# Spreading ScalarE's work over a loop, and one low half in four by TensorE and ScalarE in three stages

## The chip, the cores and the metric

The kernel runs on one core of a Trainium2 chip. The metric is the device time of one execution in microseconds (us); before the change the median of three runs is 1210.32 us (1210.09 to 1211.27).

## What is computed

A dynamic convolution over the sequence, followed by a mixture of experts with one expert per token. There are 8 x 3584 = 28672 tokens of 192 features.

```python
w = softmax(weight_gen)                       # per token and head: 7 taps
conv[b, s, h] = sum_k w[b, s, h, k] * x_pad[b, s + k, h]   # 8 heads of 24 features
logits = conv @ w_gate                        # 8 experts
e = argmax(logits);  gate = softmax(logits)[e]
out = gate * (relu(conv @ w1[e]) @ w2[e])     # 192 -> 1024 -> 192
```

## The kernel before

**Two halves of a pipeline.** The tokens are cut into 16 chunks of 14 x 128. A *producer* takes a chunk `c` through the convolution on VectorE: 14 multiplications by a tap's weight (L401) and 12 additions (L406), each over half a chunk. For the chunk before, it scales the result to float16 rows (`tops` L415 on ScalarE makes the high part, `halves` L428 on VectorE subtracts it to get the low part), transposes them on TensorE (`turn`, L442, copied out by ScalarE at L443), multiplies by the gate (`products`, L451) and routes: `route1` finds the expert and the counts, `counts` takes the exponential (L492), `route2` makes the row positions, and GpSimd scatters the rows to a list per expert in DRAM (L505). The softmax of the next chunk's tap weights (`soft_a`, `soft_e`, `soft_b`) and its size (`size_a`, L199) lie in the same loop. `load_chunk` issues the next chunk's loads on SP and copies the six positions that overlap (the halo, L119) on ScalarE.

A *consumer* works through blocks of 256 rows of one expert (stages 0 and 1 also have blocks of 128); stage `s` holds the lists filled from chunk `s`. A block of 256 has four steps. In a step `first` makes 2 x 128 hidden features with ten matmuls (L689 to L693), ScalarE applies relu and rounds to float16, the high half `hh` (L696). The rounding error, the low half `hl`, is made in one of two ways:

```python
if self.via[k]:
    PE.matmul(p1, lhsT=negi, rhs=hh, start=False, stop=True, skip_group_check=True)
    A.activation(out=hl, in_=p1, func=AF.Relu)
else:
    V.scalar_tensor_tensor(out=hl, in0=p1, scalar=0.0, in1=hh, op0=ALU.max, op1=ALU.subtract)
```

The first way takes a subtracting matmul (L703) and ScalarE (L704), the second VectorE (L706). `second` (L723) multiplies both halves by `w2`: eight matmuls for the high half and four for the low half. The low half is used four steps after its `first`. `NZ[s]` says how many of eight positions use VectorE in stage `s`; of the list `via` (L940) a block of 256 uses the first four entries. NZ is 0 for stages 0 to 4, 5 for stage 5 and 8 (VectorE alone) from there; after the producer's end VectorE takes all.

**What sets the order.** Producer and consumer are generators that yield planned times. The loop at L996 to L1002 goes on with the producer as long as its time `tp`, plus 0.65 us for each low half that VectorE was given (`own`), plus 4 us, is not beyond the consumer's time, and with the consumer otherwise. Each engine gets its instructions in the order in which this loop calls them and runs them in that order. Inside the producer, `o` counts from -1 through 13 pairs of the convolution; the tables `ZERO` to `EARLY` say at which `o` each part stands (in `EARLY`, for chunks from 4 on: tops at -1, halves at 1, turn from 2, products at 4, route1 at 6, counts at 8, route2 at 9, soft_a at 7, soft_b at 10).

Three small operations have two versions, chosen by the chunk's number: the softmax sum's epsilon (L378 on VectorE, L380 on ScalarE), the cast of the counts (L482, L484) and the gate's sum (L519, L521 with L522). On ScalarE they stand from chunk 6 on.

Of the kernel before, what the change touches and what calls it, by code (L numbers as in the profile page):

```python
# [12 lines left out]
AF = mybir.ActivationFunctionType  # L13
# [4 lines left out]
B, S, D = 8, 3584, 192  # L18
# [4 lines left out]
HALO = K - 1  # L23
T = 14
WID = [14] * 16
# [17 lines left out]
SECOND = dict(tops=-1, halves=-1, turn=-1, per=6, products=-1, route1=-1, counts=-1, route2=0, soft_a=6, soft_b=10, size=8)  # L43
END = 2.1
HEAD = 4.0
WARM = (6, 8, 18)
LONE = {1: 6, 2: 2}
WB = 4
# [7 lines left out]
HHB, HLB, YB = 6, 6, 20  # L56
AV, TLOAD, SLOW = 4.0, 12.0, 0.5
SKEW = 4.0
NZ = [0] * 5 + [5] * 1 + [8] * 10
DH = 0.65  # L60
ALWAYS = (6, 3)
REST = P
# [20 lines left out]
def conv_moe_kernel(ctx: ExitStack, tc: tile.TileContext, x, wgen, wg_in, w1, w2, out):  # L83
    nc = tc.nc
    V, A, GP, PE, SP = nc.vector, nc.scalar, nc.gpsimd, nc.tensor, nc.sync
# [15 lines left out]
    nchunk = len(WID)  # L101
# [6 lines left out]
    tin = {}  # L108

    def load_chunk(c):  # L110
        t0, w = at[c], WID[c]
        wgt = small.tile([P, T * H, K], F32, name="wgt")[:, 0:w * H, :]
        SP.dma_start(out=wgt, in_=wgen.rearrange("(p t) h k -> p t (h k)", p=P)[:, t0:t0 + w, :])
        xin = big.tile([P, (T + HALO) * D], F32, name="xin")
        z = HALO if c else 0
        for a, b in ((z, w + HALO),) if c else ((0, X0), (X0, w + HALO)):
            SP.dma_start(out=xin[:, a * D:b * D], in_=x[:, (t0 + a) * D:(t0 + b) * D])
        if c:
            A.activation(func=AF.Copy, out=xin[:, 0:HALO * D], in_=tin[c - 1]["xin"][:, WID[c - 1] * D:(WID[c - 1] + HALO) * D])  # L119
        tin[c] = dict(wgt=wgt, xin=xin)  # L120

    load_chunk(0)
    wgf = const.tile([P, 2, E], F32, name="wgf")
# [248 lines left out]
    def soft_b(c):  # L372
        wgt, n = tin[c]["wgt"], WID[c] * H
        sm = small.tile([P, T * H], F32, name="sm")[:, 0:n]
        V.tensor_reduce(out=sm, in_=wgt, axis=AX.X, op=ALU.add)
        yield 1.0
        if c < 6:
            V.tensor_scalar(out=sm, in0=sm, scalar1=1e-9, scalar2=None, op0=ALU.add)  # L378
        else:
            A.activation(out=sm, in_=sm, func=AF.Copy, bias=1e-9)  # L380
            yield None
        V.reciprocal(out=sm, in_=sm)
        yield 0.9
        V.tensor_tensor(out=wgt, in0=wgt, in1=sm.unsqueeze(2).to_broadcast([P, n, K]), op=ALU.mult)
        yield 1.0
# [71 lines left out]
    def route1(s):  # L457
        d = seg[s]
        n = WID[s]
        pl = d["pl"]  # L460
        with tc.high_priority(offset=PRIO2):
            fac = small.tile([P, 1], F32, name="fac")
            A.activation(out=fac, in_=d["sx"][:, 2:3], func=AF.Copy, scale=wi[:, 2 * E:2 * E + 1])
            lg = work.tile([P, T, E], F32, name="lg")[:, 0:n, :]
            V.tensor_reduce(out=lg, in_=pl[:, 0:16 * n].rearrange("p (t z e) -> p t e z", z=2, e=E), axis=AX.X, op=ALU.add)
            lm = small.tile([P, n], F32, name="lm")
            V.tensor_reduce(out=lm, in_=lg, axis=AX.X, op=ALU.max)
            V.tensor_tensor(out=lg, in0=lg, in1=lm.unsqueeze(2).to_broadcast([P, n, E]), op=ALU.subtract)
            vr = work.tile([P, T, E], F32, name="vr")[:, 0:n, :]
            V.scalar_tensor_tensor(out=vr, in0=lg, scalar=0.0, in1=r8.unsqueeze(1).to_broadcast([P, n, E]), op0=ALU.is_equal, op1=ALU.mult)  # L470
        yield 1.5
        with tc.high_priority(offset=PRIO2):
            ve = small.tile([P, n], F32, name="ve")
            V.tensor_reduce(out=ve, in_=vr, axis=AX.X, op=ALU.max)
            oh = work.tile([P, E * T], F32, name="oh")[:, 0:E * n].rearrange("p (e t) -> p e t", e=E)
            V.tensor_tensor(out=oh.rearrange("p e t -> p t e"), in0=vr, in1=ve.unsqueeze(2).to_broadcast([P, n, E]), op=ALU.is_equal)
            inc = work.tile([P, E * T], F32, name="inc")[:, 0:E * n].rearrange("p (e t) -> p e t", e=E)
            V.tensor_tensor_scan(out=inc.rearrange("p e t -> p (e t)"), data0=scm[n].rearrange("p e t -> p (e t)"),
                                 data1=oh.rearrange("p e t -> p (e t)"), initial=0.0, op0=ALU.mult, op1=ALU.add)
            cnt = small.tile([P, E], F16, name="cnt")  # L480
            if s < 6:
                V.tensor_copy(out=cnt, in_=inc[:, :, n - 1])  # L482
            else:
                A.activation(out=cnt, in_=inc[:, :, n - 1], func=AF.Copy)  # L484
        d.update(lg=lg, oh=oh, inc=inc, cnt=cnt, fac=fac)
        yield 1.1
# [24 lines left out]
    def route2(s):  # L511
# [3 lines left out]
        with tc.high_priority(offset=PRIO2):  # L515
            ge = small.tile([P, n], F32, name="ge")
            V.tensor_reduce(out=ge, in_=lg, axis=AX.X, op=ALU.add)
            if s < 6:
                V.tensor_scalar(out=ge, in0=ge, scalar1=1e-9, scalar2=d["sx"][:, 1:2], op0=ALU.add, op1=ALU.mult)  # L519
            else:  # L520
                A.activation(out=ge, in_=ge, func=AF.Copy, bias=1e-9)  # L521
                A.activation(out=ge, in_=ge, func=AF.Copy, scale=d["sx"][:, 1:2])  # L522
# [258 lines left out]
    def produce():  # L781

        t, ta = 10.0, 0.0
# [21 lines left out]
        for e in range(WB):  # L805
            prep_load(e)
        load_chunk(1)
        SP.dma_start(out=scri[TRASH:TRASH + 256, :].rearrange("(p j) c -> p j c", j=2), in_=zrow.bitcast(I32))
        for _ in soft_b(0):
            pass  # L810
        t += 8
        for c in range(nchunk + 1):
            dt = DT * (WID[c] if c < nchunk else T) / T
            at_o = {0: ZERO, 1: FIRST, 2: SECOND, 3: THIRD}.get(c, EARLY)
            it = conv(c) if c < nchunk else None
            tops_, turn_, products_, size_, soft_ = None, None, None, None, None
            for o in range(-1, OPS + 1 + LONE.get(c, 0) // 2):
# [7 lines left out]
                    yield t  # L825
                if o == (3 if c == 2 else 0) and c and c < nchunk - 1:
                    load_chunk(c + 1)
                if o == at_o["tops"] and c:
                    tops_ = tops(c - 1)
                for _ in range(1 if at_o in (EARLY, THIRD) else 2):  # L830
# [21 lines left out]
                for _ in range(at_o["per"]):  # L852
                    if turn_ and next(turn_, 0):
                        state["pe"] += 0.9
                        ta += 1.1
                if o == at_o["products"] and c:
                    products_ = products(c - 1)
                for _ in range(1 if at_o in (EARLY, THIRD) else 2):
# [18 lines left out]
                if c + 1 < nchunk and c != 1:  # L877
                    if o == at_o["soft_a"]:
                        ta += 1
                        for d in soft_a(c + 1):  # L880
                            t += d
                            yield t
                    if o == at_o["soft_a"] + (0 if c == 0 else 1):
                        soft_e(c + 1)
                    if o == at_o["soft_b"] and c:
                        soft_ = soft_b(c + 1)
                    while soft_ and (d := next(soft_, None)) is not None:
                        t += d
                        yield t
# [3 lines left out]
                if o == at_o["route1"] and c:  # L893
                    for d in route1(c - 1):
                        t += d
                        yield t
                if o == at_o["counts"] and c:
                    counts(c - 1)
                if o == at_o["route2"] and c == 1:
# [129 lines left out]
```

## Time and profile before

| | |
|---|---|
| median of the runs | 1210.32 us |
| profiled execution | 1210.91 us, span 1209.2 us |
| TensorE matmuls, busy | 1128.4 us (93%) |
| VectorE, busy | 1049.2 us (87%) |
| ScalarE, busy | 694.9 us (57%) |
| GpSimd, busy | 759.6 us (63%) |
| low halves by VectorE (L706) | 322, by ScalarE (L704) 134 |

Busy time is a share of the whole span, and the stages differ: the head (to about 130 us) splits the weights, in the stretch to about 480 us low halves are made by TensorE and ScalarE, then to about 1000 us by VectorE beside the convolution, and after it TensorE works on what is left of the blocks. A line number names the instruction's place in the kernel. A wait names the instruction that came last before the waiting one could begin.

### The profile page before, as it was taken

Reading aid. Unit: us, or ns where it says so; the run is one execution under the profiler, and the core shown is the slowest. Engines: PE = TensorE matmul, PEld = TensorE weight load, DVE = VectorE, ACT = ScalarE, POOL = GpSimd, SP = SyncE. Lnnn points to the kernel's source line nnn. Section 1 sums busy time; section 2 is a strip of 40 time slices with the busy share of each in tenths; the row PEclk is TensorE's granted clock in tenths of the full one; section 3 lists DMA queues with packets and bytes.
Section 4 is the critical chain, followed back from the end, with each engine's and each line's share of the span. In section 5 each row is a group of like instructions: output and inputs, shape, how many; then the busy total and the mean of one; then the engine's idle time right before and its main releaser. Section 6 shows DMA issues by size and latency. Waiting matters only on the chain.

```text
span 1209.2 us, 31966 instructions
## 1 busy us (share of the span) xinstructions
PE 1128.4 (93%) x12159; PEld 1014.2 (84%) x12159; DVE 1049.2 (87%) x1416; ACT 694.9 (57%) x1382; POOL 759.6 (63%) x587
## 2 busy tenths in 40 slices
PE   4778888999999999999999999999999999999997
PEld 3343877888878888999989999999999999999997
DVE  7999999999999999999999999999999995533332
ACT  3887657767676776755646464564646446333342
POOL 1434573847686878788838888785867875621222
PEclk9899899999999999999999999999999999999999
DMA  9987999998998999999999999999999899999994
GB/s 300 312 265 244 299 327 299 281 309 271 258 278 223 294 232 275 269 277 281 317 242 316 255 288 281 268 322 253 309 271 263 246 269 252 295 311 254 260 240 157
DMA packets 214064, 331.43 MB, mean 274 GB/s; under 512 B 138382, under 2 KB 157951, under 8 KB 211856
## 3 DMA queue, kind: packets, MB, share of 16 engines
q1 hardware_dynamic: 190752, 282.31, 84.5%
q0 software_dynamic: 21696, 44.99, 12.9%
q10 hardware_dynamic: 1456, 2.03, 0.6%
q8 instruction: 97, 1.59, 0.6%
q14 instruction: 63, 0.52, 0.2%
HBM read 246.39 MB, written 60.83 MB: 254 GB/s over the span
## 4 chain that ended last, share of the span: by engine, by line
DVE 63%; PE 23%; DMA 5%; issue 4%; ACT 3%; POOL 1%; SPq 1%; ACTq 0%; DVEq 0%; POOLq 0%
DVE acc L406 19%; DVE tmp L401 19%; PE po L723 10%; DVE hl L706 8%; DVE acc L401 3%; DVE rows L428 3%; PE p L689 2%; PE p L693 2%; PE p L692 2%; PE p L690 2%; PE p L691 2%; PE p L282 2%; DMA out_dram<-y,mt 1%; POOL out_dram L732 1%; ACT xt L443 1%
## 5 line engine op out<-in xcount | busy, mean ns | idle before, releaser
L732 POOL DMA_INDIRECT out_dram<-y,mt x228 | 318.2, 1396 | 231.1 <-ACT y L731 167.4
L505 POOL DMA_INDIRECT scr<-rows,pos x224 | 345.8, 1544 | 149.2 <-issue 57.6
L696 ACT ACTIVATE hh<-p 128x512 f16<-128x512 f32 x456 | 271.6, 598 | 259.5 <-PE p L693 252.7
L723 PE MATMUL po<-wb,hh 128*128 128x192 f16 x3648 | 359.2, 246 | 1.6 <-ACT hh L696 1.6
L706 DVE SCALAR_TENSOR_TENSOR hl<-p,hh 128x512 f16<-128x512 f32 x322 | 215.2, 678 | 116.0 <-ACT hh L696 115.7
L723 PEld LDWEIGHTS <-hh 128*128 128x128 f16 x3648 | 307.9, 98 | 4.6 <-ACT hh L696 2.2
L401 DVE TENSOR_TENSOR tmp<-xin,wgt 128x1344 f32<-128x1344 f32 x192 | 292.5, 1547 | 1.2
L406 DVE TENSOR_TENSOR acc<-acc,tmp 128x1344 f32<-128x1344 f32 x192 | 292.3, 1546 | 0.4
L689 PE MATMUL p<-xb,wa 128*128 128x256 f16 (+1 forms) x960 | 256.8, 267 | 4.8 <-DMA xb<-scr 3.9
L693 PE MATMUL p<-xb,wa 128*128 128x256 f16 (+1 forms) x960 | 256.9, 268 | 0.0
L692 PE MATMUL p<-xb,wa 128*128 128x256 f16 (+1 forms) x960 | 256.9, 268 | 0.0
L691 PE MATMUL p<-xb,wa 128*128 128x256 f16 (+1 forms) x960 | 256.8, 268 | 0.0
L690 PE MATMUL p<-xb,wa 128*128 128x256 f16 (+1 forms) x960 | 256.8, 268 | 0.0
L723 PE MATMUL po<-wb,hl 128*128 128x192 f16 x1824 | 225.5, 246 | 22.9 <-ACT hl L704 17.9
L723 PEld LDWEIGHTS <-hl 128*128 128x128 f16 x1824 | 160.0, 98 | 36.5 <-ACT hl L704 22.5
L690 PEld LDWEIGHTS <-wa 128*128 128x128 f16 x960 | 94.0, 98 | 18.9 <-issue 1.4
L704 ACT ACTIVATE hl<-p 128x512 f16<-128x512 f32 x134 | 80.9, 604 | 44.4 <-PE p L703 43.7
L689 PEld LDWEIGHTS <-wa 128*128 128x128 f16 x960 | 94.1, 98 | 10.1 <-DMA wa<-wsa 2.7
L693 PEld LDWEIGHTS <-wa 128*128 128x128 f16 x960 | 94.1, 98 | 9.8
L692 PEld LDWEIGHTS <-wa 128*128 128x128 f16 x960 | 94.1, 98 | 9.9
L691 PEld LDWEIGHTS <-wa 128*128 128x128 f16 x960 | 94.0, 98 | 9.8
L443 ACT ACTIVATE xt<-p 128x1024 f16<-128x1024 f16 x96 | 82.3, 926 | 18.7 <-PE p L442 18.6
(147 smaller groups left out, 1087.8 us busy)
## 6 DMA issues: line engine op xcount, KB each, us to landing
wb<-wsb SPq DMA_DIRECT2D x120, 768.5 KB
wa<-wsa SPq DMA_DIRECT2D x120, 768.0 KB
xin<-in_x_dram SPq DMA_DIRECT2D x15, 1344.0 KB
wa<-wsa SPq DMA_DIRECT2D x120, 128.0 KB
wgt<-in_weight_gen_dram SPq DMA_DIRECT2D x16, 392.0 KB
wa<-in_moe_w_dram SPq DMA_DIRECT2D x8, 768.0 KB
wa<-in_moe_w_dram SPq DMA_DIRECT2D x8, 512.0 KB
wsa<-wt SPq DMA_DIRECT2D x15, 256.0 KB
```

The source lines that it names most:

```text
L401: V.tensor_tensor(out=t[:, a:b, :].rearrange("p t (h g) -> p (t h) g", g=G), in0=xv, in1=wv, op=ALU.mult)
L406: V.tensor_tensor(out=acc[:, a:b, :], in0=acc[:, a:b, :], in1=t[:, a:b, :], op=ALU.add)
L505: i = raw(GP.indirect_dma_start(scri, bass.IndirectOffsetOnAxis(ap=pos[:, t:t + 1], axis=0), rows_t[s % 3].bitcast(I32)[:, t, 0:RW // 2], ...
L689: PE.matmul(o, lhsT=wt[:, F + fs:F + fs + P], rhs=xv[:, 0, :], start=i == 0, stop=False)
L690: PE.matmul(o, lhsT=wt[:, F + fs:F + fs + P], rhs=xv[:, 1, :], start=False, stop=False)
L691: PE.matmul(o, lhsT=wt[:, 3 * F + fs:3 * F + fs + P], rhs=xv[:, 0, :], start=False, stop=False)
L692: PE.matmul(o, lhsT=wt[:, 2 * F + fs:2 * F + fs + P], rhs=xv[:, 2, :], start=False, stop=False)
L693: PE.matmul(o, lhsT=wt[:, fs:fs + P], rhs=xv[:, 2, :], start=False, stop=i == self.each - 1)
L696: self.relu = raw(A.activation(out=hh, in_=p1, func=AF.Relu, scale=1.0 - 2.0 ** -11 if self.via[k] else 1.0))
L706: V.scalar_tensor_tensor(out=hl, in0=p1, scalar=0.0, in1=hh, op0=ALU.max, op1=ALU.subtract)
L723: PE.matmul(o, lhsT=h[:, js], rhs=w2, start=(f == 0 and j % 2 == 0 and not part and w == 0), stop=part == 1 and f == NF - 1 and (j % 2 == ...
L732: i = raw(GP.indirect_dma_start(out, bass.IndirectOffsetOnAxis(ap=self.mt[:, j, 1:2], axis=0), y, None, bounds_check=N - 1, oob_is_err=False))
```

## The change

The halo copy leaves `load_chunk` for a function of its own, called at `o` = 8. Before the tops, after each part of the turn and before the counts, from chunk 3 on, the producer yields a time 1.2 us later than its own, so that consumer steps may come first in the order. The exponential of the tap weights goes one place later from chunk 4 on. The three small operations stay on VectorE through chunk 7. In stages 11 to 13, `NZ` is 7 instead of 8: the first of a block's four low halves goes by L703 and L704.

```diff
@@ -43,6 +43,8 @@
 SECOND = dict(tops=-1, halves=-1, turn=-1, per=6, products=-1, route1=-1, counts=-1, route2=0, soft_a=6, soft_b=10, size=8)
 END = 2.1
 HEAD = 4.0
+HALO_AT = 8
+MORE = 1.2
 WARM = (6, 8, 18)
 LONE = {1: 6, 2: 2}
 WB = 4
@@ -56,7 +58,7 @@
 HHB, HLB, YB = 6, 6, 20
 AV, TLOAD, SLOW = 4.0, 12.0, 0.5
 SKEW = 4.0
-NZ = [0] * 5 + [5] * 1 + [8] * 10
+NZ = [0] * 5 + [5] * 1 + [8] * 5 + [7] * 3 + [8] * 2
 DH = 0.65
 ALWAYS = (6, 3)
 REST = P
@@ -115,9 +117,10 @@
         z = HALO if c else 0
         for a, b in ((z, w + HALO),) if c else ((0, X0), (X0, w + HALO)):
             SP.dma_start(out=xin[:, a * D:b * D], in_=x[:, (t0 + a) * D:(t0 + b) * D])
-        if c:
-            A.activation(func=AF.Copy, out=xin[:, 0:HALO * D], in_=tin[c - 1]["xin"][:, WID[c - 1] * D:(WID[c - 1] + HALO) * D])
         tin[c] = dict(wgt=wgt, xin=xin)
+
+    def load_halo(c):
+        A.activation(func=AF.Copy, out=tin[c]["xin"][:, 0:HALO * D], in_=tin[c - 1]["xin"][:, WID[c - 1] * D:(WID[c - 1] + HALO) * D])
 
     load_chunk(0)
     wgf = const.tile([P, 2, E], F32, name="wgf")
@@ -374,7 +377,7 @@
         sm = small.tile([P, T * H], F32, name="sm")[:, 0:n]
         V.tensor_reduce(out=sm, in_=wgt, axis=AX.X, op=ALU.add)
         yield 1.0
-        if c < 6:
+        if c < 8:
             V.tensor_scalar(out=sm, in0=sm, scalar1=1e-9, scalar2=None, op0=ALU.add)
         else:
             A.activation(out=sm, in_=sm, func=AF.Copy, bias=1e-9)
@@ -478,7 +481,7 @@
             V.tensor_tensor_scan(out=inc.rearrange("p e t -> p (e t)"), data0=scm[n].rearrange("p e t -> p (e t)"),
                                  data1=oh.rearrange("p e t -> p (e t)"), initial=0.0, op0=ALU.mult, op1=ALU.add)
             cnt = small.tile([P, E], F16, name="cnt")
-            if s < 6:
+            if s < 8:
                 V.tensor_copy(out=cnt, in_=inc[:, :, n - 1])
             else:
                 A.activation(out=cnt, in_=inc[:, :, n - 1], func=AF.Copy)
@@ -515,7 +518,7 @@
         with tc.high_priority(offset=PRIO2):
             ge = small.tile([P, n], F32, name="ge")
             V.tensor_reduce(out=ge, in_=lg, axis=AX.X, op=ALU.add)
-            if s < 6:
+            if s < 8:
                 V.tensor_scalar(out=ge, in0=ge, scalar1=1e-9, scalar2=d["sx"][:, 1:2], op0=ALU.add, op1=ALU.mult)
             else:
                 A.activation(out=ge, in_=ge, func=AF.Copy, bias=1e-9)
@@ -805,6 +808,7 @@
         for e in range(WB):
             prep_load(e)
         load_chunk(1)
+        load_halo(1)
         SP.dma_start(out=scri[TRASH:TRASH + 256, :].rearrange("(p j) c -> p j c", j=2), in_=zrow.bitcast(I32))
         for _ in soft_b(0):
             pass
@@ -825,6 +829,10 @@
                     yield t
                 if o == (3 if c == 2 else 0) and c and c < nchunk - 1:
                     load_chunk(c + 1)
+                if o == HALO_AT and c and c < nchunk - 1:
+                    load_halo(c + 1)
+                if o == at_o["tops"] and c > 2:
+                    yield t + MORE
                 if o == at_o["tops"] and c:
                     tops_ = tops(c - 1)
                 for _ in range(1 if at_o in (EARLY, THIRD) else 2):
@@ -853,6 +861,8 @@
                     if turn_ and next(turn_, 0):
                         state["pe"] += 0.9
                         ta += 1.1
+                        if c > 2:
+                            yield t + 1.2
                 if o == at_o["products"] and c:
                     products_ = products(c - 1)
                 for _ in range(1 if at_o in (EARLY, THIRD) else 2):
@@ -880,7 +890,7 @@
                         for d in soft_a(c + 1):
                             t += d
                             yield t
-                    if o == at_o["soft_a"] + (0 if c == 0 else 1):
+                    if o == at_o["soft_a"] + (0 if c == 0 else 1 if c < 4 else 2):
                         soft_e(c + 1)
                     if o == at_o["soft_b"] and c:
                         soft_ = soft_b(c + 1)
@@ -894,6 +904,8 @@
                     for d in route1(c - 1):
                         t += d
                         yield t
+                if o == at_o["counts"] and c > 2:
+                    yield t + MORE
                 if o == at_o["counts"] and c:
                     counts(c - 1)
                 if o == at_o["route2"] and c == 1:
```

The instruction orders show what moves. Line numbers of the changed kernel are 3 higher behind its new function. The first place is ScalarE at the tops (`rows`) of one of the steady chunks, at the end of its convolution. Before:

```order
L366 ACTIVATE sx<-ll 128x1
L415 ACTIVATE rows_1248<-acc,sx 128x14x128
L696 ACTIVATE hh<-p_12603 128x512
L119 ACTIVATE xin<-xin 128x1152
L415 ACTIVATE rows_1248<-acc,sx 128x14x64
L696 ACTIVATE hh<-p_12637 128x512
L681 ACTIVATE g_12656<-mt,wb_1250 128x2
```

and now:

```order
L369 ACTIVATE sx<-ll 128x1
L699 ACTIVATE hh<-p_12597 128x512
L418 ACTIVATE rows_1248<-acc,sx 128x14x128
L418 ACTIVATE rows_1248<-acc,sx 128x14x64
L699 ACTIVATE hh<-p_12634 128x512
L684 ACTIVATE g_12653<-mt,wb_1250 128x2
```

The halo copy (L119) is gone from between the two copies, and both stand behind one more high half (L696, now L699).

The second place is ScalarE at the cast of the counts of stage 14 (`cnt`), in the last chunk's convolution. Before:

```order
L696 ACTIVATE hh<-p_17234 128x512
L731 ACTIVATE y<-po,g_16974 128x192 x2
L463 ACTIVATE fac<-sx,wi 128x1
L696 ACTIVATE hh<-p_17296 128x512
L696 ACTIVATE hh<-p_17364 128x512
L484 ACTIVATE cnt<-inc 128x8
L696 ACTIVATE hh<-p_17401 128x512
L681 ACTIVATE g_17420<-mt,wb_1250 128x2
L696 ACTIVATE hh<-p_17423 128x512
L731 ACTIVATE y<-po,g_17192 128x192 x2
```

and now:

```order
L446 ACTIVATE xt<-p_17022 128x256
L699 ACTIVATE hh<-p_17072 128x512
L466 ACTIVATE fac<-sx,wi 128x1
L487 ACTIVATE cnt<-inc 128x8
L699 ACTIVATE hh<-p_17115 128x512
L707 ACTIVATE hl<-p_16954 128x512
L684 ACTIVATE g_17137<-mt,wb_1253 128x2
L699 ACTIVATE hh<-p_17141 128x512
L734 ACTIVATE y<-po,g_16877 128x192 x2
```

Behind the cast there was one high half and the gate's factor (`g`); now a low half (L707) stands there too, the one of the first step of a block.

The third place is VectorE at the routing of the same chunk, where the one-hot of the experts (`oh`) and its running sum (`inc`) are made. Before:

```order
L706 SCALAR_TENSOR_TENSOR hl<-p_17173,hh 128x512
L401 TENSOR_TENSOR tmp<-xin,wgt 128x1344
L406 TENSOR_TENSOR acc<-acc,tmp 128x1344 x2
L465 TENSOR_REDUCE lg<-route 128x112
L467 TENSOR_REDUCE lm<-lg 128x14
L468 TENSOR_TENSOR lg<-lg,lm 128x112
L470 SCALAR_TENSOR_TENSOR vr<-lg,r_105 128x112
L706 SCALAR_TENSOR_TENSOR hl<-p_17234,hh 128x512
L706 SCALAR_TENSOR_TENSOR hl<-p_17296,hh 128x512
L474 TENSOR_REDUCE ve<-vr 128x14
L476 TENSOR_TENSOR oh<-vr,ve 128x14x8
L478 SCALAR_TENSOR_TENSOR inc<-scm_125,oh 128x112
```

and now:

```order
L709 SCALAR_TENSOR_TENSOR hl<-p_16902,hh 128x512
L404 TENSOR_TENSOR tmp<-xin,wgt 128x1344 x2
L409 TENSOR_TENSOR acc<-acc,tmp 128x1344 x2
L468 TENSOR_REDUCE lg<-route 128x112
L470 TENSOR_REDUCE lm<-lg 128x14
L471 TENSOR_TENSOR lg<-lg,lm 128x112
L473 SCALAR_TENSOR_TENSOR vr<-lg,r_105 128x112
L477 TENSOR_REDUCE ve<-vr 128x14
L479 TENSOR_TENSOR oh<-vr,ve 128x14x8
L481 SCALAR_TENSOR_TENSOR inc<-scm_125,oh 128x112
L709 SCALAR_TENSOR_TENSOR hl<-p_17072,hh 128x512
L404 TENSOR_TENSOR tmp<-xin,wgt 128x1344
```

Two low halves (L706, now L709) stood in the middle of the routing; the one nearest to it now stands before the additions and the next behind the running sum. From one L428 (L431) to the next, the order has 32 low halves on VectorE in chunks 10 and 12 to 14 before (31 in chunk 11) and 27 in the last; now it has as many through chunk 12, and then 26, 21 and 18.

## Rows read from the trace of the kernel before

**Rows 1.** The page, section 4: the chain that ended last, by engine.

```profile
DVE 63%; PE 23%; DMA 5%; issue 4%; ACT 3%; POOL 1%; SPq 1%; ACTq 0%; DVEq 0%; POOLq 0%
```

**Rows 2.** Waits of VectorE, 210 to 1000 us: engine, line, releaser: us, times, longest.

```profile
DVE pos L533 <- DVE rows L530: 1.1, 7, 0.2
DVE rows L428 <- ACT rows L415: 0.7, 1, 0.7
DVE pos L533 <- DMA out_dram<-y,mt: 0.3, 2, 0.2
```

**Rows 3.** A steady chunk: stretch, its length, busy us of PE, PEld, DVE, ACT, POOL; granted clock.

```profile
867.50:938.70 71.20, 70.24 (x793) 66.35 (x791) 70.35 (x95) 36.91 (x77) 52.62 (x36) 1.00 1.04 276
```

**Rows 4.** Waits of TensorE, 210 to 960 us.

```profile
PE po L723 <- ACT hl L704: 13.5, 13, 3.4
PE po L723 <- DVE hl L706: 4.0, 7, 1.1
```

**Rows 5.** Timeline at the mark and at the end: start, us, engine, line [idle before].

```profile
962.49 1.28 DVE L706 SCALAR_TENSOR_TENSOR hl<-p,hh 128x512 f16<-128x512 f32 x2
...
963.23 0.50 PE L723 MATMUL po<-wb,hl 128*128 128x192 f16 x4 [0.97 <-DVE hl L706]
...
1201.01 0.49 PE L723 MATMUL po<-wb,hl 128*128 128x192 f16 x4
```

**Rows 6.** Waits of TensorE, 964 to 1202 us.

```profile
PE p L689 <- DMA xb<-scr: 0.6, 1, 0.6
PE route L451 <- ACT xt L443: 0.2, 1, 0.2
```

**Rows 7.** The chain in order of time, one block apart: start, us, what.

```profile
1127.70 2.31 PE po L723 x28
...
1136.03 2.31 PE po L723 x28
```

**Rows 8.** Timeline of TensorE: a subtracting matmul and the next one.

```profile
290.51 0.38 PE L703 MATMUL p<-hh,negi 128*128 128x512 f16 x1
290.72 0.27 PE L689 MATMUL p<-xb,wa 128*128 128x256 f16 x1
```

**Rows 9.** Timeline of VectorE in one chunk.

```profile
940.62 1.87 DVE L706 SCALAR_TENSOR_TENSOR hl<-p,hh 128x512 f16<-128x512 f32 x3
942.42 1.13 DVE L428 SCALAR_TENSOR_TENSOR rows<-acc,sx,rows 128x896 f16<-128x896 f32 x1
...
958.33 3.02 DVE L406 TENSOR_TENSOR acc<-acc,tmp 128x1344 f32<-128x1344 f32 x2
961.27 0.38 DVE L465 TENSOR_REDUCE lg<-route 128x112 f32<-128x224 f32 x1
...
963.69 0.26 DVE L474 TENSOR_REDUCE ve<-vr 128x14 f32<-128x112 f32 x1
...
964.68 1.53 DVE L401 TENSOR_TENSOR tmp<-xin,wgt 128x1344 f32<-128x1344 f32 x1
```

**Rows 10.** Groups of VectorE, 60 to 480 us: shapes, count | busy, mean ns.

```profile
L519 DVE TENSOR_SCALAR ge<-ge,sx 128x14 f32<-128x14 f32 x6 | 1.4, 234 | 0.2
L378 DVE TENSOR_SCALAR sm<-sm 128x112 f32<-128x112 f32 x5 | 1.1, 219 | 0.2
...
L482 DVE CAST cnt<-inc 128x8 f16<-128x8 f32 x6 | 1.0, 171 | 0.2
```

**Rows 11.** Timeline of ScalarE at chunk 6's cast of the counts.

```profile
422.28 0.22 ACT L484 ACTIVATE cnt<-inc 128x8 f16<-128x8 f32 x1 [5.14 <-DVE inc L478]
422.40 0.58 ACT L696 ACTIVATE hh<-p 128x512 f16<-128x512 f32 x1
422.88 0.59 ACT L704 ACTIVATE hl<-p 128x512 f16<-128x512 f32 x1
```

**Rows 12.** Timeline of ScalarE in the head.

```profile
109.92 0.40 ACT L270 ACTIVATE si<-idf,ws 128x128 f32<-128x128 f32 x1 [1.91 <-DVE ws L194]
...
120.05 1.79 ACT L415 ACTIVATE rows<-acc,sx 128x1792 f16<-128x1792 f32 x1 [3.41 <-DVE acc L406]
```

## The prediction

> **What bounds the kernel now.** I read the chain of waits first. It is 63% VectorE and 23% TensorE [rows 1]: VectorE sets the pace for the first four fifths, TensorE the rest. The waits of VectorE between 210 and 1000 us come next: 2.1 us in all [rows 2]. Its queue is strictly in order and never empty, so the moment at which it finishes any instruction in that stretch is the sum of the work in front of it. TensorE is nearly as full. In a steady chunk of 71.20 us it is busy for 70.24 us, VectorE for 70.35 us with small gaps between instructions [rows 3]. TensorE's waits from 210 to 960 us are led by 13.5 us for low halves made by ScalarE and 4.0 us for low halves made by VectorE [rows 4].
>
> The two engines are two queues whose relative order is fixed when the program is written. Where TensorE is the quicker one, it waits at a low half until VectorE has caught up, and whatever it gained before is lost there. So the end is set by the last such wait: VectorE's work up to it, plus TensorE's work after it. In this trace that is the low half begun at 962.49 us, for which TensorE idles 0.97 us before going on at 963.23 us [rows 5]. I call it the mark. After it TensorE waits only 0.6 us for data and 0.2 us for a copy [rows 6], and its last matmul starts at 1201.01 us [rows 5]. The same wait of about one microsecond comes once in each steady chunk, since VectorE's chunk is about one microsecond longer.
>
> **The change, part by part.** (1) *Three small operations of chunks 6 and 7 go from ScalarE to VectorE*: the sum's epsilon, the counts' cast, the gate's sum. They take 0.23, 0.22 and 0.17 us on VectorE [rows 10], so 2 x 0.62 = +1.2 us in front of the mark, with nothing to hide them. What it removes is a stall of ScalarE: in chunk 6 the cast stood 5.14 us waiting for VectorE, with high and low halves queued behind it [rows 11]. That lets TensorE arrive earlier in chunk 6 to 8, and wait longer for VectorE afterwards: 0 at the mark.
>
> (2) *ScalarE's work is spread* (the two high copies behind one more step, the halo copy six places later, the exponentials exchanged). These move ScalarE against TensorE, and no VectorE work is added. Their worth is part of the 13.5 us [rows 4], and again lies ahead of the mark. I count 0. What hides it is the DVE queue; if VectorE had idle time there, up to 13.5 us would come back, and that is a rival below. The halo copy is needed by the next chunk's first tap, some 20 us later. Chunk 2's copy goes behind weight preparation in the head; ScalarE has waits of 1.91 and 3.41 us for VectorE between there and chunk 2's first use [rows 12], more than such a copy takes, so 0 too; without that cover about +1 us. On SP every input chunk stays behind the same number of block loads, so no load is later.
>
> (3) *One low half of four in stages 11 to 13 is made by TensorE and ScalarE.* That is 7 blocks x 3 stages = 21 halves: VectorE loses 21, ScalarE gains 21, TensorE gains 21 subtracting matmuls with 512 columns of 0.21 us each, start to start [rows 8]: +4.5 us of TensorE work, which nothing can hide after the mark.
>
> The order says what VectorE does with the time given back. The planner counts 0.65 us per half as VectorE's own, and since fewer halves stand in a chunk, it puts fewer blocks beside it: 32 halves per chunk up to chunk 12 as before, then 26, 21 and 18 where there were 32, 32 and 27. So the steps go behind the mark, where TensorE alone works on them.
>
> **The sum at the last wait.** In the new order the latest wait moves to ScalarE. The counts' cast of the last chunk's routing (stage 14) waits for the scan, and right behind it stand one high half and, new, a low half that TensorE needs (the second place shown in the order). VectorE, from its start to the end of that scan, against the mark before: 188 halves instead of 208, at 0.60 us each (three in a row start 1.80 us apart from what follows [rows 9]): -12.0; the six small operations: +1.2; the reduce, the one-hot and the scan, which stood just behind the mark (963.69 to 964.68 us [rows 9]): +1.0. That is -9.8 us. Then ScalarE's cast, high half and low half, 422.28 to 423.47 us in a place like it [rows 11]: +1.2. TensorE from there to the end, counted in the two orders: 14 more first matmuls of the leading kind and 84 more second ones, which is seven steps. A block of four steps takes 8.33 us (1127.70 to 1136.03 us [rows 7]), so a step 2.08: +14.6; and 8 subtracting matmuls: +1.7. Sum: -9.8 + 1.2 + 16.3 = +7.7 us.
>
> The next candidate is VectorE's own half behind the row positions of that chunk: 15 halves fewer (-9.0), six small operations (+1.2), six tap instructions more (two take from 958.33 to 961.27 us, so 1.47 each [rows 9]: +8.8), nine routing operations at the pace of the three above (+3.0), and on TensorE 2.9 more (a first half of a step, four second matmuls, seven subtractions): +6.9. So two independent places agree on 6.9 to 7.7. The profiled execution took 1210.91 us (span 1209.2): 1218.6. The median of the runs shown is 0.6 below it, so I say 1218.0 us.
>
> Unknown is how ScalarE copes with 21 more halves of 0.6 us among its waits. From below 0: its queue has room, as the same mixture ran in stages 5 and before. From above, the worst comparable wait, 3.4 us, the longest of [rows 4], once behind the mark. I take 0, because the last chunks hold only six such halves and the nearest row is the 1.2 us of [rows 11], which is already in the sum. The ends 0 and +3.4 go to the range.
>
> **Rivals.** *Only TensorE's price*: the waits stay in sum what they were, and the end moves by 4.5 us: 1214.8. For it: in TensorE's own work that is all that is added. Against: the mark's sum says that the waits grow with the small operations. *Faster, the spread is kept*: TensorE no longer waits for ScalarE's low halves, and what it gains reaches the end: 1210.3 + 4.5 - 13.5 = 1201.3. For it: those waits are real [rows 4]. Against: TensorE waits for VectorE's halves after all of them [rows 5]. It decides if after 560 us no wait for VectorE is left; the margin to be made good is those 4.0 us [rows 4] plus the drift of about 1 us a chunk.
>
> *Faster, VectorE is relieved*: 21 x 0.60 = 12.6 us less in its queue bring the mark forward, and TensorE pays 4.5: -8.1 us, 1202.2. VectorE is busy 70.35 of 71.20 us [rows 3], so it is full. The Trainium skill (Perfetto Trace Analysis, Optimizing Scalar/DVE Operations) says that offloading to ScalarE may make sense where VectorE is saturated; by that rule the change gains, and the trace agrees that it is saturated. Against it: relief helps only if as many blocks stay ahead of the mark, and the order has 11 and 9 halves fewer in the last two chunks, not 7. *ScalarE becomes the bound*: the casts' and the gates' waits (5.14 us at one cast [rows 11]) now hold low halves in each of the last three chunks, 1 to 2 us more each on top of the forecast: 1222. *Nothing measurable*: the chunk-6 gain and the subtractions cancel, 1210 to 1212; against it stands the same argument on the mark.
>
> **How the numbers follow.** Forecast (6 to 9.5 us slower) 0.76; TensorE's price alone 0.08; ScalarE the bound 0.06; nothing measurable 0.03; the two faster ones 0.03 and 0.04. A measurement tells apart about 0.2%, 2.4 us: slower 0.76 + 0.08 + 0.06 = 0.90, same 0.03, faster 0.07. The range reaches from 1213.5, below TensorE's price, to 1220.5, part of the 3.4 us; it leaves out the faster cases, the same and most of ScalarE's, 0.16.
>
> **What would show it.** Right: 21 more subtracting matmuls, 21 fewer halves on VectorE, and VectorE still waiting some 2 us from 210 to 950 us. Steady chunks of 71.2 us to chunk 12, then about 71.2 - 6 x 0.6 = 67.6 and 71.2 - 11 x 0.6 = 64.6. ScalarE's waits at chunk 6's cast gone, TensorE's waits for ScalarE from 240 to 480 us smaller, and those for VectorE after 480 us no smaller by as much. The last wait of TensorE for a half between 945 and 970 us, at the low half behind the last chunk's cast, with about 254.6 us of TensorE work behind it, and its last matmul at about 1209 us. Wrong: VectorE idle before 950 us; a last wait before 900 us; or TensorE's work behind it grown by less than 12 us.

## The result, and the profile after

The changed kernel takes 1221.45 us (median of four runs, 1219.03 to 1221.92) where the kernel before takes 1210.51: 1.0086 of it, 95% interval 1.0068 to 1.0103. The forecast was slower, 1218.0 us with a range to 1220.5; the direction came as forecast, the size was 3.4 us short, 0.95 us beyond the range. The profiled execution took 1221.61 us (span 1219.8), 10.7 us more than the one before.

The page after, its busy line and its chain (share of the span by engine):

```profile
PE 1141.8 (94%) x12180; PEld 1024.1 (84%) x12180; DVE 1039.3 (85%) x1401; ACT 705.8 (58%) x1395; POOL 796.9 (65%) x587
...
DVE 44%; PE 37%; DMA 9%; ACT 5%; issue 3%; POOL 1%; SPq 1%; ACTq 0%; POOLq 0%; DVEq 0%
```

VectorE has 10 us less to do, TensorE 13 us more, and in the chain TensorE has 37% where it had 23% [rows 1]. Now the waits: VectorE from 210 to 950 us (engine, line, releaser: us, times, longest), answering to [rows 2]:

```profile
DVE pos L536 <- DVE rows L533: 0.6, 4, 0.2
DVE pos L536 <- DMA out_dram<-y,mt: 0.3, 2, 0.2
DVE hl L709 <- ACT hh L699: 0.3, 1, 0.3
```

VectorE still waits for no more than 1.2 us in all. TensorE's waits from 240 to 490 us, before and then after, and after from 885 us to the end, answering to [rows 4, 6]:

```profile
PE po L723 <- ACT hl L704: 13.5, 13, 3.4
PE route L451 <- ACT xt L443: 2.1, 3, 0.7
PE p L442 <- ACT xt L443: 0.6, 2, 0.3
...
PE po L726 <- ACT hl L707: 7.2, 4, 2.9
PE p L692 <- DMA xb<-scr: 4.2, 2, 2.5
PE route L454 <- ACT xt L446: 2.3, 5, 0.7
PE p L692 <- ACT xt L446: 0.6, 2, 0.3
PE p L445 <- ACT xt L446: 0.3, 1, 0.3
...
PE po L726 <- ACT hl L707: 3.3, 2, 3.1
PE route L454 <- ACT xt L446: 0.9, 1, 0.9
PE p L692 <- DMA xb<-scr: 0.4, 1, 0.4
```

The early waits for ScalarE's low halves fell from 13.5 to 7.2 us, as the spread is made for, but 4.2 us of waits for the blocks' rows (`xb`, a DMA) came in: all waits there together fell only from 16.2 to 14.6 us, and nothing of that reached the end. Late in the program there are two new waits for a low half by ScalarE. The timeline shows both: ScalarE at the cast of stage 13 (L487) and TensorE behind it, then the same for stage 14 (start, us, engine, line [idle before]):

```profile
890.44 0.22 ACT L487 ACTIVATE cnt<-inc 128x8 f16<-128x8 f32 x1 [6.81 <-DVE inc L481]
890.56 0.58 ACT L699 ACTIVATE hh<-p 128x512 f16<-128x512 f32 x1
891.04 0.59 ACT L707 ACTIVATE hl<-p 128x512 f16<-128x512 f32 x1
...
891.68 0.50 PE L726 MATMUL po<-wb,hl 128*128 128x192 f16 x4 [3.07 <-ACT hl L707]
...
955.71 0.22 ACT L487 ACTIVATE cnt<-inc 128x8 f16<-128x8 f32 x1 [3.93 <-DVE inc L481]
955.83 0.58 ACT L699 ACTIVATE hh<-p 128x512 f16<-128x512 f32 x1
956.31 0.59 ACT L707 ACTIVATE hl<-p 128x512 f16<-128x512 f32 x1
...
956.95 0.50 PE L726 MATMUL po<-wb,hl 128*128 128x192 f16 x4 [0.19 <-ACT hl L707]
...
1211.63 0.49 PE L726 MATMUL po<-wb,hl 128*128 128x192 f16 x4
```

In both places the cast waits for VectorE's scan, one high and one low half stand behind it, and TensorE stands still until that low half is there. The one of 956.95 us is TensorE's last wait for a half. After it comes TensorE's own work, 254.68 us to its last matmul, where 237.78 us stood behind the mark before [rows 5].

### The profile page after: what moved, and what is told of

The parts are those of the page before. It is cut to its first block, busy times and chain, and to the rows that moved or that the text cites. A ratio compares the mean times of both kernels' runs of the same rounds, so it can differ in the third digit from the quotient of the medians.

```text
span 1219.8 us, 32034 instructions
## 1 busy us (share of the span) xinstructions
PE 1141.8 (94%) x12180; PEld 1024.1 (84%) x12180; DVE 1039.3 (85%) x1401; ACT 705.8 (58%) x1395; POOL 796.9 (65%) x587
## 4 chain that ended last, share of the span: by engine, by line
DVE 44%; PE 37%; DMA 9%; ACT 5%; issue 3%; POOL 1%; SPq 1%; ACTq 0%; POOLq 0%; DVEq 0%
PE po L726 16%; DVE acc L409 13%; DVE tmp L404 13%; DVE hl L709 6%; PE p L692 4%; PE p L694 4%; PE p L693 4%; PE p L695 4%; PE p L696 4%; DVE rows L431 2%; DVE acc L404 2%; DMA out_dram<-y,mt 2%; DMA xb<-scr 2%; DMA wa<-in_moe_w_dram 1%; ACT xt L446 1%
## 5 line engine op out<-in xcount | busy, mean ns | idle before, releaser
L735 POOL DMA_INDIRECT out_dram<-y,mt x228 | 342.0, 1500 | 227.5 <-ACT y L734 156.2
L699 ACT ACTIVATE hh<-p 128x512 f16<-128x512 f32 x456 | 272.0, 598 | 297.6 <-PE p L696 291.3
L508 POOL DMA_INDIRECT scr<-rows,pos x224 | 361.7, 1615 | 125.4 <-issue 56.7
L709 DVE SCALAR_TENSOR_TENSOR hl<-p,hh 128x512 f16<-128x512 f32 x301 | 201.1, 679 | 133.5 <-ACT hh L699 133.4
L696 PE MATMUL p<-xb,wa 128*128 128x256 f16 (+1 forms) x960 | 258.3, 269 | 0.0
L707 ACT ACTIVATE hl<-p 128x512 f16<-128x512 f32 x155 | 93.3, 602 | 58.3 <-PE p L706 58.1
L696 PEld LDWEIGHTS <-wa 128*128 128x128 f16 x960 | 94.7, 99 | 10.3
```

The source lines that it names most:

```text
L508: i = raw(GP.indirect_dma_start(scri, bass.IndirectOffsetOnAxis(ap=pos[:, t:t + 1], axis=0), rows_t[s % 3].bitcast(I32)[:, t, 0:RW // 2], ...
L696: PE.matmul(o, lhsT=wt[:, fs:fs + P], rhs=xv[:, 2, :], start=False, stop=i == self.each - 1)
L699: self.relu = raw(A.activation(out=hh, in_=p1, func=AF.Relu, scale=1.0 - 2.0 ** -11 if self.via[k] else 1.0))
L735: i = raw(GP.indirect_dma_start(out, bass.IndirectOffsetOnAxis(ap=self.mt[:, j, 1:2], axis=0), y, None, bounds_check=N - 1, oob_is_err=False))
```

## The experiments

Ratios are to the kernel before on the same chip.

**The table alone.** The kernel before with one line of the change:

```diff
-NZ = [0] * 5 + [5] * 1 + [8] * 10
+NZ = [0] * 5 + [5] * 1 + [8] * 5 + [7] * 3 + [8] * 2
```

> The kernel before with the table NZ of the change alone, a third time, since beside both earlier series the kernel before itself took over 1245 us. Theory: 7 to 9 us slower than the kernel before, the last long wait of TensorE (2 to 3 us) at the low half behind the cast of stage 13 near 890 us. Rival A (the spread and its head are what costs): 0 to 3 us. Rival B (the subtracting matmuls' price alone): 4.5 us.

Measured: 1219.49 us (before 1210.41), 1.0069 [1.0047, 1.0091]: 8.4 us slower. The same two waits for ScalarE as in the change, of TensorE from 885 us on, and TensorE in order of time:

```profile
PE po L723 <- ACT hl L704: 3.3, 2, 3.0
PE p L689 <- DMA xb<-scr: 1.5, 1, 1.5
...
889.01 0.82 PE L723 MATMUL po<-wb,hl 128*128 128x192 f16 x4 [3.01 <-ACT hl L704]
```

So the table costs by far the larger part, and more than its 21 subtractions (4.5 us; the interval begins at 5.7).

**The spread alone.** The change with the table of before, on two chips:

```diff
-NZ = [0] * 5 + [5] * 1 + [8] * 5 + [7] * 3 + [8] * 2
+NZ = [0] * 5 + [5] * 1 + [8] * 10
```

> The change with NZ of the kernel before, a third time, with the kernel before back at 1210 us. Theory: the six small operations on VectorE and the later tops in the head are all that reaches the end: 1211.5 to 1213.5 us. Rival A (the spread is what costs the change): 1216 to 1221. Rival C (the shorter waits for ScalarE's low halves reach the end): 1203 to 1207.

Measured: 1214.61 us, 1.0027 [1.0017, 1.0038], and on another chip 1213.25 us, 1.0021 [1.0011, 1.0031]: 2.5 to 3.3 us slower, the first of them above the 1211.5 to 1213.5 us expected. It is neither the main loss nor a gain. TensorE's waits from 545 us on, in the second of these:

```profile
PE route L454 <- ACT xt L446: 4.4, 7, 0.6
PE p L692 <- DMA xb<-scr: 1.1, 1, 1.1
PE po L726 <- DVE hl L709: 0.8, 3, 0.3
```

and in the kernel before:

```profile
PE po L723 <- DVE hl L706: 5.0, 8, 1.1
PE po L723 <- ACT hh L696: 1.0, 2, 0.6
PE p L689 <- DMA xb<-scr: 0.6, 1, 0.6
PE route L451 <- ACT xt L443: 0.2, 1, 0.2
```

The wait for VectorE that came once in each steady chunk is nearly gone, and one of 0.6 us for ScalarE's copy of the transposed rows stands in its place seven times: the yields put consumer steps between the parts of the turn, and the last routing product then follows its copy more closely. In sum TensorE waits 6.3 us there instead of 6.8: it has gained next to nothing. Where the 2.5 to 3.3 us come from is taken up behind the experiments.

**The order alone.** Is it the operations of the table, or the order? In this kernel VectorE makes every low half as before; only the planner leaves the first one of each block of stages 11 to 13 out of `own`:

```diff
-                if not state["done"]:
+                if not state["done"] and not (self.light and k == 0):
                     state["own"] += DH
...
-            blk = Block(ready.pop(0), bs, via)
+            blk = Block(ready.pop(0), bs, via, light=10 < s < 14)
```

> The kernel before in which only the planner leaves the first low half of each block of stages 11 to 13 out of VectorE's own time; every instruction stays on its engine and only the order changes. Theory (the order's shift of blocks behind the last wait is the main loss): 1219 to 1224 us. Rival B (the subtractions are the price): 1209.5 to 1211.5.

Measured: 1222.32 us (before 1211.87), 1.0089 [1.0072, 1.0106]: 10.8 us slower with not one instruction added, removed or given to another engine. From one group of L428 to the next, VectorE makes 31, 28 and 25 low halves in the last three chunks instead of 32, 32 and 27, and 103 instead of 96 behind them. TensorE's waits from 885 us on:

```profile
PE po L724 <- DVE hl L707: 5.6, 3, 2.3
PE po L724 <- ACT hh L697: 2.7, 2, 1.5
```

It waits more ahead of the end, since fewer steps stand there to do, and has seven steps more behind it: 7 x 2.08 us [rows 7] = 14.6 us, less what comes earlier. The profiled execution was the longest of the four, 1227.15 us, so its waits are somewhat longer than those of the median.

**The operations alone.** The opposite: the table of the change, but every low half of stages 6 to 15 is counted as VectorE's, whoever makes it, so that the loop lays out the blocks as if nothing had been moved.

```diff
-                if not state["done"]:
-                    state["own"] += DH
+            if not state["done"] and (self.own or not self.via[k]):
+                state["own"] += DH
             self.hl[k] = hl
...
-            blk = Block(ready.pop(0), bs, via)
+            blk = Block(ready.pop(0), bs, via, own=s >= 6)
```

> The kernel before with NZ of the change, with every low half of stages 6 to 15 counted as VectorE's by the planner. Theory: as many blocks stay ahead of the last wait, and what is left is TensorE's 21 subtractions (4.5 us) less the waits that they fill: 1212 to 1214.5 us. Rival (the subtractions and ScalarE's queue are the loss, not the order): 1217 or more. Rival (the relief of VectorE brings the end forward): 1202 to 1207.

Measured: 1213.45 us (before 1211.87), 1.0010 [0.9998, 1.0022]: at most 2.7 us slower, where the table as the change has it costs 8.4. VectorE's waits from 885 to 1000 us:

```profile
DVE hl L707 <- ACT hh L697: 8.6, 7, 3.1
DVE pos L533 <- DVE rows L530: 0.3, 2, 0.2
```

VectorE now waits for ScalarE and so for TensorE, which waits for no half from 820 us on: the relief is real, and it ends where TensorE becomes the bound. The 4.5 us of subtractions mostly fill the waits for VectorE of 0.95 to 0.97 us, one in each of the last three chunks before, which are gone.

**The cast taken from ScalarE.** The change with the cast of the counts and the gate's sum of stages 11 to 15 on VectorE:

```diff
-            if s < 8:
+            if s < 8 or s > 10:
```

> The change with the counts' cast and the gate's sum of stages 11 to 15 on VectorE. Theory b1 (several places lie within 1 to 2 us of each other, so one wait gone uncovers the next): no wait of 3 us near 891 us and no lower clock after it; TensorE's last wait, 1 to 2 us, at a low half of VectorE near 970 us; 1218.5 to 1220.5 us. Theory b2 (the low half behind the cast is the loss itself): 1212 to 1216 us.

Measured: 1220.45 us, 1.0066 [1.0047, 1.0084]. TensorE's last wait for a half is now VectorE's own, the prediction's next candidate:

```profile
967.56 0.50 PE L726 MATMUL po<-wb,hl 128*128 128x192 f16 x4 [1.60 <-DVE hl L709]
```

Removing one wait uncovers the next, as theory b1 had it, with about 2 us (0.0020) between the ratios; the 1212 to 1216 us of b2 are not reached.

**The head.** In the profile of the change the tops of chunk 1 begin 1.65 us later than before, behind ScalarE's own DMA issue. ScalarE before, and after:

```profile
116.18 1.50 ACTq L300 DMA_DIRECT2D wsa<-wt  x1
...
120.05 2.72 ACT L415 ACTIVATE rows<-acc,sx 128x1792 f16<-128x1792 f32 x2 [3.41 <-DVE acc L406]
```

```profile
116.33 3.29 ACTq L303 DMA_DIRECT2D wsa<-wt  x1
...
121.70 2.72 ACT L418 ACTIVATE rows<-acc,sx 128x1792 f16<-128x1792 f32 x2 [4.96 <-issue]
```

The suspect was chunk 2's halo copy, which the change puts among the weight preparation. This puts that copy alone back, in the change (halo2) and in the spread (spread_halo2, and spread_halo2_2 on one chip with the unedited spread, spread_only_4):

```diff
                     load_chunk(c + 1)
-                if o == HALO_AT and c and c < nchunk - 1:
+                    if c == 1:
+                        load_halo(2)
+                if o == HALO_AT and 1 < c < nchunk - 1:
```

> The change with the halo copy of chunk 2 alone back where it stood (the others stay at o = 8). Theory a1 (that copy among the weight preparation delays ScalarE's DMA issue and the tops of chunk 1, and VectorE with them, by 1.7 to 2 us): tops of chunk 1 at 118.5 to 121.5 us instead of 121.7, and 1218.5 to 1220 us. Theory a2 (the issue's length varies by itself): tops as late as in the change in some runs, and 1220.5 to 1222.

> The same with NZ of the kernel before. Theory a1: what is left is the six small operations, 0.5 to 1.2 us: 1210.5 to 1212 us. Theory a2: 1212.5 to 1215, as with the copy at o = 8.

> The spread with the copy of chunk 2 where it stood. Theory a1: 0 to 1.2 us above the kernel before. Theory a2: as far above it as spread_only_4.

> The spread alone (copy of chunk 2 at o = 8), beside spread_halo2_2 on one chip. Theory a1 (the copy's place costs): 1.5 to 2.5 us above spread_halo2_2. Theory a2 (the issue varies by itself): within 1 us of it, both 0 to 2.5 us above the kernel before.

Measured: 1.0071 [1.0052, 1.0090] for the change so edited; 1.0007 [0.9992, 1.0022] and 1.0028 [1.0015, 1.0040] for the spread. On one chip the spread took 1213.25 us with the copy moved and 1213.81 with it back. So no cost of the copy's place is seen; the first two runs alone would have told the wrong story. In the profiles taken while the kernel before stood at 1210 to 1212 us, the tops of chunk 1 begin at 118.5 to 122.3 us, and with the copy back at 118.9, 121.6 and 120.1. Over all twenty profiles the first issue takes 2.5 us on the mean in the nine with the spread (1.29 to 3.34) and 1.8 us in the eleven without (1.28 to 2.62). The spread may lengthen it, but the two groups overlap; whether it does, and by which of its parts, stays open.

**Few halves, counted.** If order is the loss, a gain should be had by moving few halves and keeping the order: one low half in every eighth block of stages 6 to 12, counted as VectorE's as above, and a lead of 6 us in place of 4. These are two changes in one run, which cannot tell their shares apart.

```diff
-SKEW = 4.0
+SKEW = 6.0
...
+            if not state["done"] and (5 < s < 13 and n % 8 == 0):
+                for k in (0,):
+                    via[k] = 1
```

> The kernel before with one low half of every eighth block of stages 6 to 12 by TensorE and ScalarE, all counted as VectorE's by the planner, and the planner's lead SKEW at 6 instead of 4. Theory: VectorE is relieved of about 0.6 us in each chunk, TensorE's 0.21 us for it lies in the wait of about 1 us that it has there, and blocks that the longer lead keeps ahead of the last wait do not stand behind it: 1205 to 1208 us. Rival (each low half moved costs, wherever it stands): 1211 to 1214.

> The kernel before with one low half of every eighth block of stages 6 to 12 by TensorE and ScalarE, counted as VectorE's, and a lead of 6. Theory, after the first run (0.9977 of the kernel before): 0.1 to 0.4% faster. Rival (that run was a lucky one): within 0.1%.

Measured: 1209.38 us, 0.9977 [0.9961, 0.9993], then 1209.97 us, 0.9993 [0.9984, 1.0002]. The expected 1205 to 1208 was reached in single executions only (the profiled one, 1205.79, is the shortest). Its waits of TensorE from 540 us to the end are all but gone:

```profile
PE po L724 <- ACT hh L697: 1.6, 4, 0.6
PE po L724 <- DVE hl L707: 0.4, 2, 0.3
```

The first series points to a gain of 0.2% at the edge of what can be measured, and the second does not confirm it.

**Runs that settle nothing.** The table alone, the spread alone, the order alone and the counted table ran earlier too, the first two and the order twice, while the kernel before itself took 1246 to 1307 us beside them. Their edits are those above; these are their expectations:

> The kernel before with the table NZ of the change alone. Theory (blocks move behind the last wait, and ScalarE's cast of the counts holds a low half): TensorE's last long wait, 2 to 3 us, stands at the low half behind the cast of stage 13, near 890 us; no head loss; 1217 to 1219 us. Rival A (the spread of ScalarE's work and its head are what costs): 1210 to 1213. Rival B (the subtracting matmuls' price and no more, 21 x 0.21 us): 1214.8.

> The change with NZ of the kernel before (spread, halo copy and small operations alone). Theory: VectorE's six small operations (1.2 us, of which about half comes back) and the later tops in the head (1.7 to 1.9 us) are all that reaches the end: 1211.5 to 1213.5 us; the steady chunks stay at 71.2 us. Rival A (the spread is what costs): 1216 to 1221. Rival C (the shorter waits for ScalarE's low halves reach the end): 1203 to 1207.

> The kernel before, in which the planner leaves the first low half of each block of stages 11 to 13 out of VectorE's own time, as the change makes it, while VectorE still makes it. No work is added or taken away; only the order changes. Theory (the order's shift of blocks behind the last wait is the main loss): slower by 9 to 13 us, 1219 to 1224, more than the change itself, since VectorE is not relieved. Rival B (the subtractions are the price): within 1 us of the kernel before, 1209.5 to 1211.5.

> The kernel before with NZ of the change, in which the planner counts every low half of stages 6 to 15 as VectorE's, whoever makes it, so that as many blocks stay ahead of the last wait. Theory: the order keeps its 32 low halves' places per chunk, VectorE is relieved, and what is left is TensorE's 21 subtractions (4.5 us) less the waits of about 1 us per chunk which they fill: 1212 to 1214.5 us, with VectorE waiting for ScalarE between 900 and 1000 us. Rival (the subtractions and ScalarE's queue are the loss, not the order): 1217 or more. Rival (the relief of VectorE brings the end forward): 1202 to 1207.

> The same kernel again, because the kernel before itself took 1246 to 1274 us beside the first series. Theory (the order's shift of blocks behind the last wait is the main loss): slower than the kernel before by 9 to 13 us. Rival B (the subtractions are the price): within 1 us of it.

> The same kernel again, for the same reason. Theory: the last long wait of TensorE, 2 to 3 us, at the low half behind the cast of stage 13 near 890 us, and 7 to 9 us slower than the kernel before. Rival A (the spread and its head are what costs): 0 to 3 us. Rival B (the subtracting matmuls' price alone): 4.5 us.

> The change with NZ of the kernel before, again, since the kernel before itself took over 1245 us beside the first series. Theory: the six small operations on VectorE and the later tops in the head are all that reaches the end: 1 to 3 us slower than the kernel before. Rival A (the spread is what costs the change): 6 to 11 us slower. Rival C (the shorter waits for ScalarE's low halves reach the end): 3 to 7 us faster.

Measured, as ratios to that slower kernel before: 1.0041 and 1.0001 for the table, 1.0281 and 1.0442 for the spread, 1.0111 and 1.0044 for the order, 1.0107 for the counted table. What they show of the changes is lost in what disturbed the kernel before by 3 to 8%, and nothing here rests on them.

## Why the prediction was right in kind and short in size

**The bound.** Right: VectorE waits for 1.2 us in all from 210 to 950 us. What TensorE gained between 240 and 490 us, 16.2 - 14.6 = 1.6 us of waits, was nearly gone at its first wait for VectorE behind it, 1.41 us at 539.47 us.

**The order.** Right: the steady chunks of VectorE, from one group of L431 to the next, are 70.1 to 71.1 us up to chunk 12 and then 67.5 and 65.1 us; forecast were 67.6 and 64.6. The order alone, without its operations, is as slow as the whole change.

**The last wait.** Right in place: at the low half behind the last chunk's cast, at 956.95 us, within the 945 to 970 us of the forecast. From cast to that half 1.24 us passed; 1.2 were forecast.

**The sum there.** This is the step that was mis-sized, in VectorE's term above all:

| from the mark (963.23 us) to the last wait | forecast | measured |
|---|---|---|
| VectorE to the end of the scan | -9.8 | 955.71 - 963.23 = -7.5 |
| cast, high half, low half | +1.2 | 956.95 - 955.71 = +1.2 |
| TensorE behind it | +16.3 | 254.68 - 237.78 = +16.9 |
| sum | +7.7 | +10.6 |

The prediction's "about 254.6 us" of TensorE work behind the wait is a slip: its own terms give 237.78 + 16.3 = 254.1. VectorE's term is 2.3 us short. Of these, 1.65 us are there at chunk 1 already, as the tops in the head show, and VectorE keeps them: it begins the halves of chunk 4 (L431, before L428) at 243.97 us instead of 242.15. I had costed the head at 0 because ScalarE had idle time of 1.9 and 3.4 us there [rows 12]; but the longer of these holds ScalarE's own DMA issues, which the profile does not count as busy and whose length varies, so it was no cover. In the table alone, with its tops at 119.97 us and without the 1.2 us of small operations, the same place is at 954.12 us and the last matmul at 1209.37 us. With chunk 2's halo copy back (halo2), where VectorE is at the halves of chunk 4 at 242.15 us as before the change, the cast of stage 14 begins at 954.01 us, 1.7 us sooner than in the change. So the head is most of what the term lacked. How much of it is the change and how much this one execution is open, as the head's issue varies by as much between executions; without these 1.65 us the profiled time would have been 1220.0, inside the range. The other 0.6 us stands in no row that I can name; the table alone lacks as much (its cast begins at 952.88 us, where the prediction's terms without the small operations give 963.23 - 11.0 = 952.2). Of TensorE's 0.6 us, 0.5 are the waits for data and copies behind the last wait (1.3 us in the change, 0.8 before).

**The spread at 0.** Too low: alone it costs 2.5 to 3.3 us against the 1.2 us of the small operations. Its profile on the second chip (1214.63 us, 3.7 more than before) shows where: TensorE's last wait for VectorE, and before the change the matmul that has as many behind it; then VectorE at the halves of one chunk, each time the spread first (start, us, engine, line):

```profile
771.65 0.50 PE L726 MATMUL po<-wb,hl 128*128 128x192 f16 x4 [0.25 <-DVE hl L709]
...
768.44 0.49 PE L723 MATMUL po<-wb,hl 128*128 128x192 f16 x4
...
728.71 2.07 DVE L431 SCALAR_TENSOR_TENSOR rows<-acc,sx,rows 128x1792 f16<-128x1792 f32 x1
...
725.18 2.07 DVE L428 SCALAR_TENSOR_TENSOR rows<-acc,sx,rows 128x1792 f16<-128x1792 f32 x1
```

At that wait 3.2 of the 3.7 us are there already (on the first chip, by the same count, 4.1 of 5.7). VectorE is 3.5 us late, and 2.45 of these stand at the halves of chunk 4 (244.60 against 242.15 us), ahead of the small operations: the head again, and the 1.2 us. The 0.6 us waits for the copies only stand where TensorE waited for VectorE before; the 3.2 us do not come from them. How much of the late head is the spread's own stays open, as said above.

**The candidate I did not list.** The low half behind stage 13's cast, 3.07 us of waiting, is as late as the forecast's place: TensorE came from it to 956.95 us with only 0.19 us of waiting left. Taking both casts off ScalarE uncovered a wait of 1.60 us for VectorE, as that run shows.

**The rivals.** "Only TensorE's price" (1214.8) falls with the table alone at 1219.5 and with the counted table at 1.0010. The relief falls as the change stands: VectorE's queue is shorter by 10 us of work, and the end is later. By the Trainium skill (Perfetto Trace Analysis, Optimizing Scalar/DVE Operations), offloading work to ScalarE may make sense where VectorE is saturated; the trace agrees that VectorE was relieved, by 10 us of busy time. The counted table shows what was missing: an order that keeps as many steps ahead of the last wait. "ScalarE the bound" (1222) is the nearest in time, but its mechanism, a further microsecond or two in each of three chunks, is not in the trace: the second cast adds 0.19 us behind the first one's 3.07.

## What to carry to other kernels

Where one planner both gives work to engines and orders it by their load, moving an operation changes the order of everything else, and that can cost more than the operation: count the moved work at its old price first, and see what is left. Compare the sums "work of the engine that is ahead, up to its last wait, plus work of the other one behind it" in the old and the new order; that needs only the order and durations of the old trace. And where two places are within a microsecond of each other, taking one wait away shows the next. Before idle time is counted as cover, look at what the engine's queue did in it: ScalarE's idle time in the head was its own DMA issues.

## What the runs showed of the hardware that was not expected

TensorE's clock fell after the 3.07 us of idling at stage 13. The stretch before it, the one behind it and the next (length, busy us of PE, PEld, DVE, ACT, POOL; granted clock, DMA share, GB/s):

```profile
860.00:891.00 31.00, 28.62 (x347) 26.66 (x344) 30.80 (x33) 15.98 (x29) 28.14 (x11) 1.00 1.04 294
891.70:896.40 4.70, 4.70 (x34) 4.03 (x35) 4.70 (x6) 1.85 (x6) 3.87 (x6) 0.64 1.14 186
896.40:900.00 3.60, 3.60 (x39) 3.26 (x37) 3.60 (x4) 2.02 (x5) 2.99 (x3) 1.00 0.36 108
```

and TensorE in order of time within it:

```profile
893.83 0.42 PE L692 MATMUL p<-xb,wa 128*128 128x256 f16 x1
894.04 0.42 PE L693 MATMUL p<-xb,wa 128*128 128x256 f16 x1
```

First matmuls start 0.21 us apart instead of 0.11: the lower level, 1.2 GHz, for a part of these 4.7 us. At 0.64 of the full clock that is 0.36 x 4.70 = 1.7 us of TensorE's work. It did not move the end here, since TensorE then met the next wait with 0.19 us to spare; it would have to be counted where no such wait follows.

The length of the wait alone does not tell when this happens. The steady chunk of [rows 3], with a wait of 0.96 us, has 1.00. In the change the clock stayed at 1.00 behind a wait of 2.57 us that ended at 446.78 us, and fell behind waits of 1.41 and 0.55 us that ended at 539.47 and 541.19 us:

```profile
446.00:449.00 3.00, 2.22 (x22) 1.99 (x23) 2.96 (x4) 3.00 (x7) 2.69 (x2) 1.00 0.21 33
449.00:452.00 3.00, 3.00 (x35) 2.78 (x33) 3.00 (x3) 2.42 (x9) 2.39 (x3) 1.00 0.99 384
...
543.00:546.00 3.00, 3.00 (x25) 2.44 (x23) 3.00 (x5) 0.60 (x1) 2.39 (x3) 0.72 0.98 178
```

And an issue of one DMA by ScalarE is not a fixed price: the first of them at the end of the head took 1.28 to 3.34 us in twenty profiles.
